# Batch 0's first heads and mixed k rows: the maximum as the bias of the exponentials, v only cast, and a new order

## The chip, the core and the metric

The kernel runs on one core of a Trainium2 chip. The metric is the device time of one launch in microseconds. The core's engines run side by side, each working through its own queue in order: TensorE (PE; its weight loads are listed as PEld), VectorE (DVE), ScalarE (ACT), GpSimd (POOL) and SyncE (SP), which only issues transfers. Matmul results land in PSUM, 8 banks of 128 x 512 fp32; the kernel numbers them 0 to 7.

## What is computed

Two stages. The first is an attention without a softmax over pairs: queries and keys are mapped by a small matrix to 128 features, and the features and their negatives go through an exponential, each row lowered by its largest absolute value. The second is a feed-forward with a gate.

```python
def phi(x):                                   # x: (8, 8, 576, 64), w_phi: (64, 128)
    proj = np.einsum('bhsd,df->bhsf', x, w_phi)
    proj = proj - np.max(np.abs(proj), axis=-1, keepdims=True)
    return np.concatenate([np.exp(proj), np.exp(-proj)], axis=-1)
q_p, k_p = (phi(q), phi(k))
kv = np.einsum('bhsf,bhsd->bhfd', k_p, v)
z = np.sum(k_p, axis=2)
num = np.einsum('bhsf,bhfd->bhsd', q_p, kv)
den = np.einsum('bhsf,bhf->bhs', q_p, z)[..., None] + 1e-06
attn = num / den
...
x = attn as (4608, 512)                       # tokens x (heads * 64)
gate = np.maximum(x @ w_gate, 0.0)            # (512, 1536)
val = x @ w_val                               # (512, 1536)
out = gate * val @ w_out                      # (4608, 512), fp32
```

In `phi`, one maximum m per row of k stands in both halves: exp(p - m) and exp(-p + m). Since these are factors of a whole row, exp(-m) and exp(m) may as well be multiplied onto the row of v that the row of k meets in `kv`.

## The kernel before

The program is a list of short steps, written out in the string `ORDER` (lines 17 to 256) and carried out word by word: `ke.0.1.3.0:6@kp1` is step ke with arguments 0, 1, 3, 0, PSUM bank 6, and buffer 1 of ring kp. The list's order is each engine's order; the engines meet only at the data and buffers that they share.

Batches are worked one after the other. Of each head's 576 rows, 512 are taken as four blocks of 128; the last 64 rows of all heads are the mixed rows. k is worked in three groups of heads, (0, 1), (2, 3, 4), (5, 6, 7), where the first group has the mixed rows in its free place. The feed-forward works on groups of 512 tokens: groups 0 to 7 for the batches, and group 8 for the mixed rows. There the steps are, with the lines of the profile:

- Loads: `lf` is the first k load; `lk`, `lq`, `lv`, `lm`, `lw` load k, q, v and their mixed rows (GpSimd issues those of k and q, and batch 0's v; SyncE issues the later v and the mixed v); `wl` (L532) loads a third of one feed-forward weight, wv or wg.
- k of batch b, group j, block i: features (`k3` or `kr`, L566), then `kx` (L670) takes the largest absolute value of each row on DVE, and `ke` (L662) the two exponentials on ACT, for all three heads at once, 384 columns, sign s = 0 or 1. `ke` does not lower by the maximum. Instead `kk` (L679) makes exp(-m) and exp(m) of the maxima (12 columns), and GpSimd multiplies v by both (`vs`, L719, with `vo` for the column of ones that gives z; `vq` for mixed rows).
- For batch 0's first group this is done on DVE and through PSUM: `kp` (L690) writes exp(-m) and exp(m) into a PSUM bank, `vd` (L700, two of them) multiplies v by them, `vp` (L709) writes the column of ones, and `vz` (L652, two of them) multiplies the mixed rows of v.
- `kv` (L768) are the products of k's exponentials and the scaled v; `kc` (L779) copies them out on ACT, once for each group of heads.
- q: features (`qb` or `qc`), exponentials `qe` (L843, ACT, 512 columns), and the maximum by `qx`, `qy`, `qz`, `qu` (DVE, with a transpose on TensorE) and `qw` (L884, ACT, a small exponential for each token block of batch 0).
- Output of attention for token block i, head group g: `nu` (L891, matmuls of 65 columns), `nt` and `nv` (L912, L922, DVE), the reciprocal `nr` (L930, DVE), and the normalization `nx` (L934, GpSimd).
- The transposed activations: for batch 0 by TensorE, `xp` (L971), and a copy, `xa` (L985, ACT) or `xc` (DVE); for later batches by a transposing transfer of SyncE.
- Feed-forward of group 0 in quarters: `pv`, `pg` (L1094), `pa` (L1109, ACT), `pb` (L1115, DVE). Of the others: `fv`, `fg` (L1065), `va` or `vb` (L1080, L1083), `ga` (L1086), and the output products `fo` (L1126), copied out by `oc` (L1135, ACT) or `oe` (DVE) and stored by `od`. One row block is done in halves at the end: `fp` (L1157), `o1` (L1166) and `d1` (L1173) on ACT, `o2`, `d2` on DVE and SyncE.
- `zz.N` (L429) are N matmuls of zeros into bank 7, whose result is not used.

## Time and profile before

| | |
|---|---|
| time, median of 3 runs | 372.36 us (372.12 to 373.22) |
| the profiled execution: its time | 371.86 us |
| the profiled execution: its span | 370.1 us |
| instructions | 9178 |
| PE busy | 362.3 us, 98% of the span |
| PEld busy | 196.8 us, 53% |
| DVE busy | 289.2 us, 78% |
| ACT busy | 227.1 us, 61% |
| POOL busy | 156.5 us, 42% |
| granted TensorE clock | 1.00 |
| HBM | 37.81 MB read, 9.44 MB written |

The span runs from the first to the last recorded instruction or transfer; 1.8 us of the execution lie around it. Ends of matmuls are modelled in the profile and matmuls overlap, so PE's busy time says how long some matmul was open. In a timeline the columns are start, duration, engine, line, operation and tiles, and how many instructions one row merges; in square brackets stands how long the engine was idle before and what ended it. A row of the waits reads: who, for whom; us in total, times, longest.

### The profile page before, as it was taken

The numbers are of one execution on the slowest core, as the hardware profiler recorded it, in microseconds if no ns is written. First come the engines' busy times: TensorE is split into PE (matmuls) and PEld (weight loads), VectorE is DVE, ScalarE is ACT, GpSimd is POOL, SyncE is SP. The second block draws the span as 40 slices with busy tenths as digits, with TensorE's granted clock in tenths as the row PEclk, the third lists the DMA queues.
The fourth block names the chain that finished last, engine by engine and source line by source line (L and its number), as shares of the span: only waits on it lengthen the run. The fifth ranks groups of instructions, "written<-read, shape, count | busy, mean of one in ns | idle before, by whom it ended". The sixth has DMA issues, their size and how long they took to land.

```text
span 370.1 us, 9178 instructions
## 1 busy us (share of the span) xinstructions
PE 362.3 (98%) x3573; PEld 196.8 (53%) x3624; DVE 289.2 (78%) x674; ACT 227.1 (61%) x550; POOL 156.5 (42%) x161
## 2 busy tenths in 40 slices
...
GB/s 144 253 197 196 178 186 142 182 16 171 135 108 123 158 130 76 83 173 100 58 102 116 14 144 57 46 113 58 126 69 15 2 73 97 47 0 25 33 28 142
DMA packets 90380, 38.09 MB, mean 103 GB/s; under 512 B 64226, under 2 KB 85602, under 8 KB 90338
## 3 DMA queue, kind: packets, MB, share of 16 engines
...
q8 instruction: 28, 0.46, 0.5%
q10 hardware_dynamic: 144, 0.13, 0.1%
...
HBM read 37.81 MB, written 9.44 MB: 128 GB/s over the span
## 4 chain that ended last, share of the span: by engine, by line
PE 87%; issue 4%; DVE 4%; POOL 2%; ACT 1%; DMA 1%; SPq 0%; POOLq 0%; ACTq 0%
PE bank L1065 43%; PE bank L1126 22%; PE bank L768 4%; PE bank L1094 4%; PE bank L891 4%; PE bank L566 2%; PE bank L828 2%; PE bank L429 2%; POOL xu L934 1%; ACT kp L662 1%; DVE h L851 1%; PE bank L1047 1%; PE bank L1157 1%; DMA xTs<-xu 1%; DVE kT L550 1%
## 5 line engine op out<-in xcount | busy, mean ns | idle before, releaser
L1126 PE MATMUL bank<-wo,h 128*128 128x512 bf16 x401 | 96.2, 379 | 1.1 <-issue 0.2
L662 ACT ACTIVATE kp<-bank 128x384 bf16<-128x384 f32 x192 | 84.4, 518 | 15.1 <-PE bank L566 10.1
L1080 ACT CAST val<-bank 128x512 bf16<-128x512 f32 x81 | 47.2, 595 | 73.7 <-PE bank L1065 65.1
L1086 DVE SCALAR_TENSOR_TENSOR h<-bank,val 128x512 bf16<-128x512 f32 x100 | 66.8, 678 | 28.1 <-PE bank L1065 14.2
L1065 PE MATMUL bank<-xTs,wv 128*128 128x512 bf16 x334 | 85.6, 379 | 0.8
L1065 PE MATMUL bank<-xTs,wg 128*128 128x512 bf16 x340 | 85.3, 379 | 0.6
L934 POOL TENSOR_TENSOR xu<-u,r 128x512 bf16<-128x512 f32 x36 | 37.2, 1041 | 96.0 <-DVE r L930 48.1
L843 ACT ACTIVATE qp<-bank 128x512 bf16<-128x512 f32 x128 | 69.2, 620 | 10.7 <-PE bank L828 9.4
L719 POOL TENSOR_TENSOR vs<-vn,ek 128x780 bf16<-128x780 f32 (+2 forms) x40 | 53.7, 1363 | 24.6 <-ACT ek L679 13.5
L1126 PEld LDWEIGHTS <-h 128*128 128x128 bf16 x420 | 39.1, 98 | 45.8 <-issue 2.4
L1065 PEld LDWEIGHTS <-wg 128*128 128x128 bf16 x400 | 37.4, 98 | 41.3 <-issue 0.7
L1065 PEld LDWEIGHTS <-wv 128*128 128x128 bf16 x400 | 36.9, 98 | 40.4 <-issue 0.7
L670 DVE TENSOR_REDUCE mk<-bank 128x3 f32<-128x384 f32 x96 | 49.6, 540 | 2.4 <-ACT kp L662 1.3
L851 DVE TRANSPOSE_TENSOR_REDUCE maxq<-bank 128x16 f32<-128x512 f32 x56 | 37.4, 692 | 6.1 <-ACT qp L843 3.3
L922 DVE TENSOR_TENSOR u<-bank,t 128x195 f32<-128x195 f32 (+1 forms) x108 | 33.8, 329 | 2.8 <-POOL xu L934 0.6
L912 DVE TENSOR_TENSOR t<-bank,cq 128x195 f32<-128x195 f32 (+1 forms) x96 | 30.1, 324 | 6.8 <-PE bank L891 5.9
L891 PEld LDWEIGHTS <-qp 128*128 128x128 bf16 x512 | 23.1, 98 | 12.6 <-issue 2.0
L891 PE MATMUL bank<-kv,qp 128*128 128x65 bf16 x512 | 26.1, 193 | 0.4 <-ACT kv L779 0.2
L1135 ACT COPY ob<-bank 128x512 f32<-128x512 f32 x19 | 11.3, 596 | 22.2 <-PE bank L1126 22.1
L747 POOL TENSOR_TENSOR vr<-vm,ek 64x520 bf16<-64x520 f32 x14 | 14.8, 1057 | 21.3 <-DMA vm<-in_v_dram 10.6
L1138 DVE COPY ob<-bank 128x512 f32<-128x512 f32 x16 | 11.0, 685 | 16.1 <-PE bank L1126 13.8
L768 PEld LDWEIGHTS <-kp 128*128 128x128 bf16 x640 | 21.6, 97 | 2.8 <-ACT qp L843 0.2
...
## 6 DMA issues: line engine op xcount, KB each, us to landing
out_dram<-ob SPq DMA_DIRECT2D x31, 256.0 KB, 2.4
vn<-in_v_dram SPq DMA_DIRECT2D x24, 256.0 KB, 4.4
...
out_dram<-ob SPq DMA_DIRECT2D x9, 128.0 KB, 2.3
```

The costliest lines, as they stand in the source:

```text
L662: nc.scalar.activation(kp_of(3 * b + j)[:, i, s].rearrange("p n f -> p (n f)"), bank[bk[0]][:, 0 : 3 * F], AF.Exp, scale=(1.0, -1.0)[s],)
L670: nc.vector.tensor_reduce(mk_of(3 * b + j)[:, :, i], bank[bk[0]][:, 0 : 3 * F].rearrange("p (n f) -> p n f", f=F), axis=AX.X, op=ALU.max, ...
L719: nc.gpsimd.tensor_tensor(vs_of(3 * b + j)[:, s, 0:n].rearrange("p n i e -> p (n i) e")[:, :, 0:e], src[:, lo:hi].rearrange("p h i e -> p ...
L768: nc.tensor.matmul(out_ps[:, h - lo, s, :], lhsT=lhsT, rhs=rhs, start=(at == 0), stop=(at == 2 * n * (C + 1) - 1),)
L843: nc.scalar.activation(qp_of(4 * b + i)[:, s, 4 * hq : 4 * hq + 4].rearrange("p h m -> p (h m)"), bank[bk[0]], AF.Exp, scale=(1.0, -1.0)[s],)
L851: nc.vector.tensor_reduce((maxq0[:, i] if b == 0 else maxq)[:, :, i, 4 * hq : 4 * hq + 4].rearrange("p t h -> p h t"), bank[bk[0]].rearran ...
L891: nc.tensor.matmul(bank[bk[0]][:, E * n : E * (n + 1)], lhsT=qp_of(4 * b + i)[:, s, h, :], rhs=kv_of(b)[:, h, s, 0:E],)
L934: eng.tensor_tensor(xu_of(n).rearrange("p (h d) -> p h d", d=D), u_of(n)[:, :, 0:D], r_of(n).to_broadcast([P, H, D]), op=ALU.mult,)
L1065: nc.tensor.matmul(bank[bk[0]], lhsT=w[:, dc, P * f : P * f + P], rhs=xT(g)[:, dc, :], start=(dc == 0), stop=(dc == NDC - 1),)
L1080: nc.scalar.copy(val_of(NFC * g + f), bank[bk[0]])
L1086: nc.vector.scalar_tensor_tensor(h2_of(g, f), bank[bk[0]], 0.0, val_of(NFC * g + f), op0=ALU.max, op1=ALU.mult)
L1126: nc.tensor.matmul(bank[bk[0]], lhsT=h2_of(g, f)[:, P * t : P * t + P], rhs=wo_sb[:, f, :], start=(f == 0), stop=(f == NFC - 1),)
```

## The change

For batch 0's first group of heads, with the mixed rows, the maximum goes into the exponentials themselves. `kb` (DVE) makes the negated maxima of the group, 12 columns. Each `ke` of the group becomes a `kz`: three exponentials on ACT, one for each head, 128 columns each, with the row's maximum as bias (-m with sign 0, m with sign 1). v of the group is then the same for both signs: `vc` (DVE) casts it once, `vi` (DVE) sets the column of ones, and `vk` (DVE, two of them) copies the mixed rows. `kp`, `vd`, `vp` and `vz` go. `kv` reads the one plane of v for both signs. Other groups and batches are computed as before.

The memset of the mixed v (`ms.2`) now covers two columns, the first of which the load `lw` of the mixed v then writes over, so that this load comes behind the memset; in the order it stands behind the fourth maximum of the second group. The whole list is in a new order. In it batch 0's v is loaded after all of its q and k; the v of batch 1 and the last third-loads of the weights (`wl`) stand elsewhere; `w1` and `wa`, which make a second form of the feature matrix, come later; the filler is 88 matmuls in 19 places instead of 85 in 22; and the last row block is `fo.7.0` with `oc` and `od` instead of the half block `fp.7.2.0` with `o1` and `d1`.

The list is shown to a little beyond the first `pv`, and at its end:

```diff
 ORDER = """
-ms.0 lf ms.2 lm.0.0 ms.4@vr0 ms.6 id lk.0.2 lk.0.0 wq ms.3@vr1 if ms.5 zz.15:7 kf.0:0 ms.9 kf.1:1
-zz.6:7 wd kh.0:0@kT0 sl k3.1.0:23 ke.0.1.0.0:2@kp0 w1:4 kg.1:1 kx.0.1.1:3@mk0 kx.0.1.0:2 wa:4 zz.2:7
-k3.1.1:56 ke.0.1.3.0:6 lm.0.1 kx.0.1.2:5 zz.3:7 k0.2:0 lq.0.1 ke.0.1.3.1:6 k1.2:0@kT1 ke.0.1.0.1:2
-zz.3:7 k0.0:1 ke.0.1.2.1:5 ke.0.1.1.1:3 k3.2.1:42 ke.0.1.2.0:5 kx.0.1.3:6 k1.0:1@kT2 zz.5:7
-k3.0.1:06 kk.0.1.0@ek0 k3.0.0:15 ke.0.1.1.0:3 ke.0.0.3.0:6@kp1 q0.1:3 lw.0.1 lq.0.0 kx.0.2.3:2@mk1
-kx.0.2.2:4 kk.0.1.1 ke.0.2.2.0:4@kp2 kx.0.0.0:1@mk2 kx.0.0.2:0 lv.0.1 ke.0.2.2.1:4 ke.0.0.1.1:5
-kx.0.0.3:6 q1.1:3@qT0 ke.0.0.1.0:5 ke.0.0.3.1:6 lv.0.0 zz.6:7 q0.0:4 kx.0.0.1:5 wl.0.1 zz.4:7
-k3.2.0:36 lv.0.2 ke.0.2.3.0:2 ke.0.0.2.1:0 ke.0.0.0.1:1 q1.0:4@qT1 ke.0.2.3.1:2 kx.0.2.1:6 zz.1:7
-qb.1.1:5 zz.3:7 qb.0.1:4 kx.0.2.0:3 ke.0.0.0.0:1 zz.2:7 qb.0.0:2 qx.0.0.1:4 ke.0.0.2.0:0 zz.1:7
-qb.1.0:1 qx.0.1.1:5 zz.7:7 qy.0.1:0 kp.0.0.0:2 ke.0.2.0.0:3 lk.1.3 kk.0.2.1@ek1 lw.0.0 kp.0.0.1:2
-kk.0.2.0 ke.0.2.1.1:6 vo.1@vs0 qx.0.1.0:1 qe.0.0.1.0:4@qp0 ke.0.2.0.1:3 qe.0.0.1.1:4 lq.1.2
-qe.0.1.0.0:1@qp1 qe.0.1.0.1:1 vs.0.1.0 qz.0.1:0@my0 zz.4:7 qb.0.3:0 qx.0.0.0:2 zz.2:7 qy.0.0:3
-vd.0.0.0:2@vs1 qz.0.0:3@my1 vs.0.1.1 qe.0.1.1.1:5 vp.0:2 qu.0.1@mz0 ke.0.2.1.0:6 qe.0.1.1.0:5 wl.0.0
-vz.0:2 qb.0.2:4 zz.2:7 qb.1.3:3 zz.2:7 qb.1.2:1 vd.0.0.1:2 qu.0.0@mz1 vz.1:2 qe.0.1.3.0:3@qp2
-vo.2@vs2 qw.0.0@cq0 qx.0.0.3:0 qx.0.0.2:4 qe.0.0.0.0:2 vs.0.2.1 zz.7:7 kv.0.0:6 qx.0.1.3:3 lw.1.1
-vs.0.2.0 kc.0.0:6@kv0 kt.1.1@kT3 qe.0.0.0.1:2 kv.0.2:5 kv.0.1:6 qe.0.0.2.1:4@qp3 lm.1.1 kc.0.2:5
-wl.1.1 kc.0.1:6 nu.0.0.0:2 nt.0.0.0:2@t0 zz.1:7 nu.0.0.2:5 qw.0.1 qx.0.1.2:1 qe.0.0.2.0:4
-qe.0.1.3.1:3 nu.0.0.1:6 nv.0.0.0:2@u0 zz.2:7 nu.0.1.2:4 lv.1.2 nu.0.1.0:2 qe.0.1.2.1:1 nt.0.0.1:6@t1
-lm.1.0 nt.0.0.2:5@t2 qy.0.2:3 nv.0.0.1:6 qe.0.0.3.0:0 nv.0.0.2:5 nt.0.1.0:2@t3 zz.2:7 nu.0.1.1:6
-qy.0.3:5 nr.0.0@r0 qe.0.1.2.0:1 qz.0.2:3@my2 nv.0.1.0:2@u1 qz.0.3:5@my0 qu.0.2@mz2 zz.5:7
-kr.1.1:3125 qe.0.0.3.1:0 nt.0.1.2:4@t0 nt.0.1.1:6@t1 qw.0.2 wl.1.0 nu.0.2.2:0 nx.0.0@xu0 nv.0.1.2:4
-xp.0.0:7 nv.0.1.1:6 nt.0.2.2:0@t2 ke.1.1.3.1:5@kp3 nr.0.1@r1 nu.0.2.1:4 xa.0.0:7 nt.0.2.1:4@t3
-nu.0.2.0:6 ke.1.1.0.1:3 nt.0.2.0:6@t0 qu.0.3@mz1 ke.1.1.0.0:3 pv.1.0:7 nv.0.2.1:4@u2 nv.0.2.2:0
-nv.0.2.0:6 nu.0.3.1:4 qw.0.3 ke.1.1.1.0:1 nx.0.1@xu1 kx.1.1.0:3@mk3 xp.0.1:0 pa.1.0:7@val0
-kx.1.1.3:5 pv.0.0:6 nr.0.2@r2 xa.0.1:0 nt.0.3.1:4@t1 nu.0.3.0:3 kx.1.1.1:1 nt.0.3.0:3@t3
+ms.0 ms.6 id ms.3@vr0 lf lk.0.0 wq ms.4@vr1 lm.0.1 sl if zz.15:7 kf.1:0 kf.0:1 lm.0.0 ms.9
+kg.1:0@kT0 kh.0:1 wd zz.6:7 k3.1.0:23 ms.5 zz.2:7 k3.1.1:45 lq.0.1 vi.0@vs0 ke.0.1.1.1:3@kp0 kx.0.1.0:2@mk0
+ke.0.1.1.0:3 ke.0.1.0.1:2 ke.0.1.3.0:5 kx.0.1.2:4 kx.0.1.1:3 lk.0.2 zz.4:7 k0.0:6 k1.0:6@kT1 lq.0.0
+kx.0.1.3:5 ms.2 lw.0.0 lw.0.1 zz.6:7 k3.0.0:01 kx.0.0.0:0@mk1 ke.0.1.2.1:4 k3.0.1:36 ke.0.1.2.0:4 kx.0.0.3:6
+ke.0.1.0.0:2 kk.0.1.1@ek0 zz.7:7 k0.2:4 kx.0.0.1:1 lv.0.1 ke.0.1.3.1:5 kz.0.0.0.1:0@kp1 kz.0.0.3.1:6
+q0.1:2 lv.0.2 kx.0.0.2:3 k1.2:4@kT2 kb.0 zz.4:7 k3.2.1:54 kk.0.1.0 kz.0.0.1.1:1 kz.0.0.2.1:3
+kz.0.0.2.0:3 q1.1:2@qT0 zz.3:7 q0.0:2 lv.0.0 kx.0.2.3:4@mk2 kx.0.2.2:5 qb.1.1:3 lm.1.1
+kz.0.0.0.0:0 q1.0:2@qT1 qx.0.1.1:3 kz.0.0.3.0:6 qb.1.0:0 ke.0.2.3.1:4@kp2 zz.4:7 k3.2.0:62 wl.0.1
+kz.0.0.1.0:1 ke.0.2.3.0:4 zz.3:7 qb.0.1:1 lk.1.3 kx.0.2.1:2 wl.0.0 ke.0.2.2.1:5 lm.1.0
+qe.0.1.0.1:0@qp0 kx.0.2.0:6 qx.0.0.1:1 ke.0.2.2.0:5 vk.1 kk.0.2.1@ek1 vc.0 lq.1.2 zz.10:7 qy.0.1:4
+qz.0.1:4@my0 qb.1.2:5 kk.0.2.0 qe.0.1.0.0:0 ke.0.2.0.1:6 ke.0.2.0.0:6 qx.0.1.0:0 qe.0.1.1.0:3@qp1
+qu.0.1@mz0 zz.3:7 qb.0.0:4 zz.3:7 qb.0.3:0 qe.0.0.1.1:1 qx.0.0.0:4 qe.0.0.1.0:1 qe.0.1.1.1:3
+ke.0.2.1.0:2 qb.1.3:6 qx.0.1.3:6 ke.0.2.1.1:2 vs.0.1.1@vs1 zz.8:7 qy.0.0:1 qx.0.1.2:5 qw.0.1@cq0
+qz.0.0:1@my1 vs.0.1.0 vs.0.2.0@vs2 qe.0.0.0.1:4 vo.1 qe.0.0.0.0:4 vk.0 zz.1:7 qb.0.2:3 lw.1.0
+qu.0.0@mz1 vo.2 vs.0.2.1 qx.0.0.3:0 kv.0.0:1 kc.0.0:1@kv0 qx.0.0.2:3 kv.0.1:2 qy.0.2:4
+qe.0.1.2.1:5@qp2 kv.0.2:1 qw.0.0 kt.1.1@kT3 qe.0.1.2.0:5 qz.0.2:4@my2 nu.0.0.0:4 kt.1.2@kT1
+nt.0.0.0:4@t0 kc.0.1:2 lw.1.1 qy.0.3:5 qz.0.3:5@my0 zz.1:7 nu.0.0.1:2 nv.0.0.0:4@u0 qu.0.2@mz2
+kc.0.2:1 qe.0.1.3.0:6@qp3 qw.0.2 lv.1.1 nt.0.0.1:2@t1 nu.0.0.2:5 nt.0.0.2:5@t2 nv.0.0.1:2 nu.0.1.1:1
+wl.1.1 nv.0.0.2:5 qu.0.3@mz0 nu.0.1.2:4 nr.0.0@r0 qe.0.0.2.1:3 nt.0.1.1:1@t3 nt.0.1.2:4@t0 zz.3:7
+nu.0.1.0:2 nv.0.1.1:1@u1 qe.0.0.2.0:3 qe.0.0.3.1:0 nt.0.1.0:2@t1 qe.0.0.3.0:0 w1:5 wa:5 nu.0.2.1:3
+nv.0.1.2:4 nv.0.1.0:2 zz.4:7 nu.0.2.0:1 nt.0.2.0:1@t2 nx.0.0@xu0 nt.0.2.1:3@t3 qe.0.1.3.1:6 qw.0.3
+zz.1:7 xp.0.0:7 kr.1.1:0542 xa.0.0:7 nu.0.3.2:6 nv.0.2.0:1@u2 nr.0.1@r1 nv.0.2.1:3 nt.0.3.2:6@t0
+nu.0.3.0:1 nu.0.2.2:7 ke.1.1.3.0:2@kp3 nt.0.2.2:7@t1 nv.0.3.2:6@u0 ke.1.1.0.0:0 ke.1.1.3.1:2
+nv.0.2.2:7 pv.0.0:3 nt.0.3.0:1@t2 ke.1.1.1.0:5 kx.1.1.3:2@mk3 nr.0.2@r2 nx.0.1@xu1 nv.0.3.0:1
+qt.1.1@qT2 nx.0.2@xu2 xp.0.1:6 ke.1.1.0.1:0 pv.1.0:7 kx.1.1.0:0 xa.0.1:6 nu.0.3.1:2 ke.1.1.1.1:5
+wl.1.0 pv.1.1:1 nt.0.3.1:2@t3 pa.1.0:7@val0 xp.0.2:6 pv.0.1:7 ln.0.0 pa.0.0:3@val1 kx.1.1.1:5
+nv.0.3.1:2 pa.1.1:1@val2 ku.1@kT2 ke.1.1.2.0:4 qc.1.1:3015 nr.0.3@r0 xa.0.2:6 nx.0.3@xu3 lm.2.0
 ...
-fo.7.0.1:2 fo.7.0.2:2 fp.7.2.1:0 oc.7.0:2@ob1 od.7.0 od.8.0 fo.7.1.0:4 fo.7.1.1:4 fo.7.3.2:1
-fo.7.1.2:4 oe.7.3:1@ob2 fp.7.2.0:6 od.7.3 oe.7.1:4@ob1 o2.7.2:0@ob0 od.7.1 d2.7.2 o1.7.2:6 d1.7.2
+ga.7.6:2@hs9 ga.7.11:7@hs7 fo.7.1.0:0 oe.8.1:4@ob0 od.6.0 fp.7.2.0:3 fo.7.1.1:0 o1.7.2:3@ob2 od.8.2
+oc.8.0:5@ob1 fo.7.3.0:6 d1.7.2 fo.7.3.1:6 fp.7.2.1:1 fo.7.3.2:6 o2.7.2:1 od.8.1 od.8.0 oe.7.3:6@ob0
+d2.7.2 fo.7.1.2:0 oe.7.1:0@ob1 od.7.1 fo.7.0.0:2 od.7.3 fo.7.0.1:2 fo.7.0.2:2 oc.7.0:2@ob2 od.7.0
 """
...
+    mneg = sb.tile([P, 3, 3, 4], FP32, name="mneg", tag="mneg")
...
+    BIASED = (0,)
...
-            2: lambda: nc.vector.memset(vm_of(0)[:, :, D : D + 1], 1.0),
+            2: lambda: nc.vector.memset(vm_of(0)[:, :, D - 1 : D + 1], 1.0),
...
+    def do_kb(bk, j):
+        nc.vector.tensor_scalar_mul(
+            mneg[:, j].rearrange("p n i -> p (n i)"), mk_of(j).rearrange("p n i -> p (n i)"), -1.0
+        )
+
+    def do_kz(bk, b, j, i, s):
+        for n in range(3):
+            nc.scalar.activation(
+                kp_of(j)[:, i, s, n],
+                bank[bk[0]][:, F * n : F * (n + 1)],
+                AF.Exp,
+                bias=(mneg[:, j] if s == 0 else mk_of(j))[:, n, i : i + 1],
+                scale=(1.0, -1.0)[s],
+            )
+
+    def cast_v(copy, j):
+        lo, hi = HEADS[j]
+        copy(
+            vs_of(j)[:, 0, 0 : hi - lo].rearrange("p n i e -> p (n i) e")[:, :, 0:D],
+            v_flat()[:, lo:hi].rearrange("p h i e -> p (h i) e"),
+        )
+
+    def do_vc(bk, j):
+        cast_v(nc.vector.tensor_copy, j)
...
+    def do_vi(bk, j):
+        n = HEADS[j][1] - HEADS[j][0]
+        nc.vector.memset(vs_of(j)[:, 0, 0:n].rearrange("p n i e -> p (n i) e")[:, :, D : D + 1], 1.0)
...
+    def do_vk(bk, hh):
+        r = slice(SM * hh, SM * (hh + 1))
+        nc.vector.tensor_copy(vr_of(0)[r, 0, :, hh, 0:E], vm_of(0)[r])
...
                 for i in range(C + 1):
                     if i < C:
                         lhsT = kp_of(3 * b + j)[:, i, s, 3 - n + h - lo, :]
-                        rhs = vs_of(3 * b + j)[:, s, h - lo, i, 0:E]
+                        plane = 0 if b == 0 and j in BIASED else s
+                        rhs = vs_of(3 * b + j)[:, plane, h - lo, i, 0:E]
                     else:
                         lhsT = kp_of(3 * b)[:, h // 2, s, 0, :]
-                        rhs = vr_of(b)[:, s, h // 2, h % 2, 0:E]
+                        rhs = vr_of(b)[:, s if b else 0, h // 2, h % 2, 0:E]
```

428 lines of the change are left out of this document (215 added, 213 removed).

## The prediction

> **What bounds the kernel now.** I read the page's chain that ended last first, then the busy time by stretches, then the waits of each engine inside a stretch, and last the timeline of the queue that the change loads.
>
> ```profile
> PE 87%; issue 4%; DVE 4%; POOL 2%; ACT 1%; DMA 1%; SPq 0%; POOLq 0%; ACTq 0%
> ```
>
> Over the whole span the chain is TensorE's. But the change sits in the first 25 us, so the stretches count more than the sums. Columns of the next rows: PE, PEld, DVE, ACT, POOL busy, granted clock, DMA share, GB/s.
>
> ```profile
> 0.00:10.00 10.00, 8.94 (x82) 6.57 (x84) 6.38 (x18) 5.03 (x12) 8.88 (x17) 1.00 0.97 149
> 10.00:20.00 10.00, 9.84 (x81) 5.54 (x76) 9.80 (x23) 9.96 (x29) 7.82 (x9) 1.00 1.27 248
> 20.00:28.00 8.00, 7.50 (x174) 6.36 (x172) 7.94 (x26) 7.71 (x20) 4.47 (x7) 1.00 1.28 197
> 28.00:40.00 12.00, 12.00 (x234) 11.24 (x234) 11.92 (x31) 11.80 (x29) 8.30 (x11) 1.00 1.09 185
> ```
>
> TensorE's busy share before 28 us is mostly the filler matmuls on zeros, so it says nothing there. ACT (9.96 of 10) and DVE (9.80 of 10) are both full from 10 to 20 us. Who waited, in three answers: ACT from 6.7 to 27.4 us, DVE from 6.7 to 25.6, PE's matmuls from 28 to 366:
>
> ```profile
> ACT kp L662 <- PE bank L642: 1.1, 1, 1.1
> ACT kp L662 <- PE bank L566: 0.2, 1, 0.2
> ```
>
> ```profile
> DVE my L869 <- PE bank L861: 0.2, 1, 0.2
> ```
>
> ```profile
> PE bank L1094 <- ACT xTs L985: 0.2, 1, 0.2
> PE bank L1126 <- issue: 0.2, 1, 0.2
> ```
>
> The 1.1 is before the first exponential. After it ACT waits 0.2 us until 27.4 and DVE 0.2 us until 25.6: two queues that run end to end. From 28 us on the matmuls wait 0.4 us in 338. So the time is (when TensorE gets its first feed-forward work) + (a fixed amount of matmul work without gaps) + (the tail). An edit at the start moves the end one for one, and the body has almost nothing to give.
>
> The first feed-forward matmuls (step pv) wait for the transposed activations that ACT copies out (xa.0.0). ACT's and TensorE's timelines at that place:
>
> ```profile
> 26.36 0.21 ACT L884 ACTIVATE cq<-mz 128x8 f32<-128x8 f32 x1
> 26.80 0.49 ACT L662 ACTIVATE kp<-bank 128x384 bf16<-128x384 f32 x1 [0.23 <-PE bank L566]
> 27.31 0.58 ACT L985 COPY xTs<-bank 128x512 bf16<-128x512 bf16 x1
> ```
>
> ```profile
> 27.95 1.05 PE L1094 MATMUL bank<-xTs,wv 128*128 128x128 bf16 x16 [0.24 <-ACT xTs L985]
> 28.84 0.34 PE L891 MATMUL bank<-kv,qp 128*128 128x65 bf16 x6
> ...
> 30.14 0.47 PE L891 MATMUL bank<-kv,qp 128*128 128x65 bf16 x10
> 30.44 0.22 PE L1094 MATMUL bank<-xTs,wv 128*128 128x128 bf16 x1
> ```
>
> **ACT, part by part.** The terms come from the groups on ACT between 6.7 and 27.3 us, and from its timeline:
>
> ```profile
> L662 ACT ACTIVATE kp<-bank 128x384 bf16<-128x384 f32 x25 | 10.5, 549 | 1.3 <-PE bank L642 1.1 <-PE bank L566 0.2
> ...
> L679 ACT ACTIVATE ek<-mk 128x12 f32<-128x12 f32 x4 | 0.9, 234 | 0.0
> ```
>
> ```profile
> 10.66 4.38 ACT L662 ACTIVATE kp<-bank 128x384 bf16<-128x384 f32 x11
> 15.08 0.18 ACT L690 ACTIVATE bank<-mk 128x12 f32<-128x12 f32 x1
> 15.20 0.47 ACT L662 ACTIVATE kp<-bank 128x384 bf16<-128x384 f32 x1
> ```
>
> Neighbours overlap, so a queue is priced by its step, not by the mean duration. Eleven exponentials of 384 columns take 4.38, one alone 0.47: the step is (4.38 - 0.47)/10 = 0.39. A 12-column one steps 15.20 - 15.08 = 0.12. Removed: 8 steps ke.0.0 x 0.39 = 3.12, and 2 steps kp x 0.12 = 0.24; together 3.36.
>
> Added: 8 steps kz, each three exponentials of 128 columns with a bias column, 24 in all. No exponential of before takes its bias from a tile, so this cost is bounded. Lower end, the overlapped step: 0.12 + 116 columns x (0.39 - 0.12)/372 = 0.20. Upper end, nothing overlapped: the means, 0.234 + 116 x (0.549 - 0.234)/372 = 0.33. I take 0.29, nearer to the upper end: each of the 24 must fetch its own column of maxima before its data can run, and the overlap that makes the lower end was seen only where nothing is fetched. 24 x 0.29 = 6.96 (ends 4.8 and 7.9). Net on ACT +3.6 (ends +1.4 and +4.5).
>
> The Trainium skill, page "ScalarE: Activation LUTs", section "What ACT_TABLE_LOAD costs", has a rule that speaks against this change: an ACTIVATE pays about 93 ns more for a bias read through a [128,1] pointer than for an immediate, on top of a fixed part and 0.833 ns per column, and neighbours overlap by about 93 ns. By its figures a kz exponential would be an estimated 0.29 us with the pointer and 0.20 without, and the net on ACT +3.7 or +1.4. No run here shows the pointer's part yet.
>
> Of what stands ahead of xa.0.0 on ACT, two things more change: batch 1's first exponential goes behind it (-0.39; it is the 25th of the group row), and the last of batch 0's four query scales (qw.0.3) goes ahead (+0.12). 3.6 - 0.27 = +3.3; the 0.2 that ACT waited at 26.80 is swallowed: **+3.1** (ends +0.9 and +4.0). w1 and wa are moved but stay ahead of xa.0.0: nothing.
>
> New waits on ACT: kz with sign 0 waits for kb (all four maxima, negated), with sign 1 for its own maximum; every later exponential queues behind. The order puts kk and ke.0.1 steps between and the sign-1 steps first, and a DVE maximum (0.55 in the first row below) is shorter than the three exponentials that it frees (0.87), so I cost it at nothing; if a maximum is late, one such step, 0.55.
>
> **DVE.** Groups of DVE from 6.7 to 25.5 us, and the reciprocal that opens the first normalization:
>
> ```profile
> L670 DVE TENSOR_REDUCE mk<-bank 128x3 f32<-128x384 f32 x12 | 6.0, 549 | 0.0
> ...
> L652 DVE TENSOR_TENSOR vr<-vm,bank 64x520 bf16<-64x520 f32 x2 | 1.4, 676 | 0.0
> L700 DVE TENSOR_TENSOR vs<-vn,bank 128x512 bf16<-128x512 f32 x2 | 1.3, 660 | 0.0
> ```
>
> ```profile
> 25.49 0.17 DVE L930 RECIPROCAL r<-u 128x8 f32<-128x8 f32 x1
> ```
>
> Removed 1.4 + 1.3 = 2.7 (and vp, a cast of 16 columns). Added: one cast of v (512 wide), two of 260 on 64 rows, one negation of 12. A cast is at most the multiply that it replaces (0.66, 0.68, 0.68) and none is under the 8-column reciprocal, 0.17, which I take for the negation: 0.7 to 2.2, and I take 1.3, near the middle, as the two narrow ones are half as wide as their multiply. So DVE is relieved by 1.4 (0.5 to 2.0). That is worth nothing on the path if ACT is 3 us behind: the second half of kv goes through ACT's copies (kc.0.1, kc.0.2), which stand behind all of the batch-0 exponentials, and the first ratio on DVE needs them. DVE's gain becomes idle time.
>
> **TensorE, GpSimd, loads.** Ahead of the first pv the new order has nu.0.3.2 and nu.0.3.0, 10 matmuls of 65 columns that before come after it: (30.44 - 30.14)/10 = 0.03 each, **-0.3**. Filler: 88 instead of 85, in idle time, nothing. After the first pv ACT does five k exponentials and xa.0.1 (5 x 0.39 + 0.58 = 2.5) while TensorE has two pv (27.95 to 28.84 is one, 0.9), the transposes and six nu matmuls (2.2): **+0.3** of idle that the row of before doesn't have. The v loads of batch 0 stand behind the same q and k loads in both orders; those of batch 1 feed only GpSimd. SyncE's load of the mixed v now waits for a memset behind four maxima on DVE (2.2 us of them); behind it on SyncE queue only mixed v and batch 1's v, and its reader stands eight maxima and four copies further on: nothing, unless it lands after DVE asks. GpSimd issues fifteen loads ahead of its four v multiplies; the groups of GpSimd up to 26.8 us:
>
> ```profile
> L719 POOL TENSOR_TENSOR vs<-vn,ek 128x768 bf16<-128x768 f32 x4 | 5.8, 1476 | 0.0
> L438 POOL DMA_DIRECT2D kn<-in_k_dram x3 | 2.5, 823 | 0.0
> ```
>
> 15 x 0.82 + 5.8 = 18, from some 2 us on: near 21, an estimate, while ACT's batch-0 work then runs to about 27. Nothing.
>
> **The tail.** Before, the last work is a 256-wide product, ACT's half copy and a 128 KB store; after, it is a full row block (fo.7.0, oc.7.0, od.7.0). ACT's last rows, and the stores issued after 300 us (KB, median us to landing):
>
> ```profile
> 360.85 0.58 ACT L1135 COPY ob<-bank 128x512 f32<-128x512 f32 x1 [3.73 <-PE bank L1126]
> 366.97 0.37 ACT L1166 COPY ob<-bank 128x256 f32<-128x256 f32 x1 [5.53 <-PE bank L1157]
> 367.37 0.37 ACTq L1173 DMA_DIRECT2D out_dram<-ob  x1
> ```
>
> ```profile
> out_dram<-ob SPq DMA_DIRECT2D x8, 256.0 KB, 2.2
> out_dram<-ob SPq DMA_DIRECT2D x9, 128.0 KB, 2.3
> out_dram<-ob ACTq DMA_DIRECT2D x1, 128.0 KB, 1.8
> ```
>
> The copy grows by 0.58 - 0.37 = 0.2, the store by up to 2.2 - 1.8 = 0.4: **+0.5** (0.2 to 0.6).
>
> **The sum.** +3.1 - 0.3 + 0.3 + 0.5 = +3.6 on the profiled execution's 371.86, that is 375.5. That execution lies 0.5 below the median of the three runs, 372.36; against the median the forecast is **376.0**, +1.0%. With kz at its ends the same sum is +1.4 and +4.5, 373.8 and 376.9. (About 0.3%, 1.1 us, is what a measurement of this kernel can tell from no change: 371.2 to 373.5.)
>
> **Rivals.** One: kz is cheap, 0.20, and ACT still paces. 373.8, right above the border of no change. For it: all ACT rows of before overlap well. Against: none of them reads a bias. 0.23.
>
> Two, the other side: ACT isn't what is late, DVE is, and the change relieves it. Place: the reciprocal at 25.49. DVE's queue ahead of it loses 1.4 and gains steps moved forward (one k transpose and the smaller max steps of two more token blocks, some 1.3), less one ratio; so it comes some 0.4 to 1.0 earlier, the first pv with it, no idle after it: -0.7 - 0.3 + 0.5 = -0.5, 371.9, and 371.0 with the small tail and the large relief. For it: DVE is as full as ACT (7.94 of 8 from 20 to 28). It decides only where the kz work costs no more than what it replaces less DVE's gain, 24 x 0.12 = 2.9, below the lower end of 0.20. 0.18, a part of which is that my reading of the ACT queue is wrong.
>
> Three: the forecast, and a weight load comes late too. The last third of wv:
>
> ```profile
> 35.35 0.82 POOL L532 DMA_DIRECT2D wv<-in_moe_w_val_dram  x1
> ```
>
> ```profile
> DMA to landing us min/median/max: 6.4/8.0/11.0
> ```
>
> ```profile
> 44.39 1.03 PE L1065 MATMUL bank<-xTs,wv 128*128 128x512 bf16 x3
> ```
>
> Its first reader came 9.0 after the issue. In the new order three more load issues (0.7 each) stand between the last normalization of batch 0 and this one, so 6.9 remain, against a landing of 8.0 in the median: a wait of 1.1 (none to 4), 377.1. 0.13.
>
> **How the numbers follow.** Forecast 0.46, one 0.23, two 0.18, three 0.13. Faster by over 0.3%: two thirds of rival two, 0.12. Within 0.3%: the rest of it and 0.09 of rival one, 0.15. Slower: 0.73. The range reaches from rival two's 372.0 (leaving out its faster part) to 377.6, the forecast with kz at 0.33 and half of rival three's wait; some 0.07 lies above.
>
> **What would show it.** Right: the kz step from a run of them, 0.27 to 0.31; ACT without waits until xa.0.0, which starts near 30.4; DVE with some 2 to 3 us of waits for PE and ACT between 7 and 28; first pv near 31; matmul waits after it under 1.5; a last ACT copy of 0.58. Wrong: kz steps near 0.20 (rival one); xa.0.0 at or before 27.3 with ACT waiting (rival two); a wait for wv near 47 us (rival three); matmul waits of several us in the body, which none of my terms holds.

## The result and the profile after

The changed kernel takes 374.99 us (median of 6 executions, 373.75 to 376.12), the kernel before 372.44 beside it (6 executions, 371.95 to 373.22): a ratio of 1.0072 [1.0059, 1.0086]. The profiled execution took 374.90 us, its span is 373.1. That is slower, as forecast (376.0), and inside the range. But the experiments below show that the size came out right with a part of the working wrong: a second limit, VectorE's casts against GpSimd, lies right behind ScalarE's longer queue, and the queues that the prediction priced one by one hold each other up. The prediction had neither.

The page's chain that ended last, first part, and the busy time of two stretches (PE, PEld, DVE, ACT, POOL busy, granted clock, DMA share, GB/s):

```profile
PE 94%; ACT 2%; DVE 2%; issue 1%
```

```profile
10.00:20.00 10.00, 8.33 (x66) 4.68 (x64) 7.98 (x14) 10.00 (x36) 7.86 (x8) 0.83 1.25 241
20.00:28.00 8.00, 7.35 (x135) 5.58 (x135) 7.88 (x23) 6.97 (x18) 2.47 (x4) 1.00 1.34 205
```

By the chain TensorE looks even more like the limit than before (94% for 87%), and again the start decides. ScalarE is full from 10 to 20 us, as before. Two things are new: VectorE has 2.0 us of idle time there, and TensorE's granted clock is 0.83, where the kernel before had 1.00 all through. The longest waits of ACT, DVE and PE between 6.7 and 28 us, and of PE from 28 to 370:

```profile
ACT kv L822 <- DVE h L894: 0.9, 1, 0.9
```

```profile
DVE mk L712 <- PE bank L644: 1.4, 2, 1.1
DVE h L894 <- PE bank L857: 0.8, 2, 0.6
```

```profile
PE bank L857 <- ACT kp L670: 1.4, 2, 1.0
```

```profile
PE bank L1169 <- issue: 0.6, 4, 0.2
```

A ring can be read out of the first three: TensorE's query matmuls (L857) wait for PSUM banks that the new exponentials (L670) hold, VectorE waits for TensorE, and ScalarE's copy of kv waits for VectorE. After 28 us nothing waits to speak of. The first feed-forward matmuls start here:

```profile
30.88 1.05 PE L1137 MATMUL bank<-xTs,wv 128*128 128x128 bf16 x16
```

30.88 against 27.95, 2.93 later, while the profiled executions differ by 3.04. What follows the first pv takes 374.90 - 30.88 = 344.02 us here and 371.86 - 27.95 = 343.91 before. In all twelve kernels below it is 343.97 to 344.5. So all but some 0.6 us of any difference in this document is made ahead of the first pv.

### The profile page after: what moved, and what is told of

It reads as the page before. It is cut to its first block, busy times and chain, and to the rows that moved or that the text cites. A ratio compares the mean times of both kernels' runs of the same rounds, so it can differ in the third digit from the quotient of the medians.

```text
span 373.1 us, 9209 instructions
## 1 busy us (share of the span) xinstructions
PE 362.9 (97%) x3575; PEld 196.8 (53%) x3627; DVE 287.5 (77%) x674; ACT 229.9 (62%) x564; POOL 156.2 (42%) x161
## 4 chain that ended last, share of the span: by engine, by line
PE 94%; ACT 2%; DVE 2%; issue 1%
PE bank L1108 46%; PE bank L1169 24%; PE bank L811 5%; PE bank L934 4%; PE bank L1137 4%; PE bank L568 3%; PE bank L871 2%; PE bank L431 2%; ACT kp L670 1%; DVE h L894 1%; ACT kp L704 1%; PE bank L1200 1%; PE bank L1090 1%; PE bank L857 0%; DVE vs L680 0%
## 5 line engine op out<-in xcount | busy, mean ns | idle before, releaser
L1169 PE MATMUL bank<-wo,h 128*128 128x512 bf16 x402 | 97.4, 379 | 1.3 <-issue 0.6
L704 ACT ACTIVATE kp<-bank 128x384 bf16<-128x384 f32 x184 | 83.2, 534 | 11.7 <-PE bank L568 8.4
L1108 PE MATMUL bank<-xTs,wg 128*128 128x512 bf16 x339 | 86.3, 379 | 0.7
L886 ACT ACTIVATE qp<-bank 128x512 bf16<-128x512 f32 x128 | 71.3, 658 | 8.6 <-DVE maxq L894 5.3
L811 PE MATMUL bank<-vs,kp 128*128 128x65 bf16 x512 | 22.3, 193 | 0.1
L811 PE MATMUL bank<-vr,kp 128*128 128x65 bf16 x128 | 20.3, 193 | 0.0
```

What stands on the lines that cost most here:

```text
L704: nc.scalar.activation(kp_of(3 * b + j)[:, i, s].rearrange("p n f -> p (n f)"), bank[bk[0]][:, 0 : 3 * F], AF.Exp, scale=(1.0, -1.0)[s],)
L811: nc.tensor.matmul(out_ps[:, h - lo, s, :], lhsT=lhsT, rhs=rhs, start=(at == 0), stop=(at == 2 * n * (C + 1) - 1),)
L886: nc.scalar.activation(qp_of(4 * b + i)[:, s, 4 * hq : 4 * hq + 4].rearrange("p h m -> p (h m)"), bank[bk[0]], AF.Exp, scale=(1.0, -1.0)[s],)
L1108: nc.tensor.matmul(bank[bk[0]], lhsT=w[:, dc, P * f : P * f + P], rhs=xT(g)[:, dc, :], start=(dc == 0), stop=(dc == NDC - 1),)
L1169: nc.tensor.matmul(bank[bk[0]], lhsT=h2_of(g, f)[:, P * t : P * t + P], rhs=wo_sb[:, f, :], start=(f == 0), stop=(f == NFC - 1),)
```

## The experiments

Four theories met in the first four runs. One: ScalarE's queue got longer, and sets the first pv. Two: VectorE is late, through the cast of v. Three: the fall of TensorE's clock costs the time. Four: the new order costs it, whatever the method. This table holds all twelve runs; each time is a median of 4 to 12 executions, each ratio is to the kernel before on the same chip, and the last three columns are of the profiled execution (its time, the start of its first pv, its mean granted clock).

| kernel | us | ratio [95%] | profiled us | first pv | clock |
|---|---|---|---|---|---|
| before | 372.44 | | 371.86 | 27.95 | 1.000 |
| changed | 374.99 | 1.0072 [1.0059, 1.0086] | 374.90 | 30.88 | 0.995 |
| old_method | 375.89 | 1.0095 [1.0067, 1.0123] | 376.82 | 32.85 | 0.990 |
| one_wide | 378.30 | 1.0155 [1.0130, 1.0180] | 378.53 | 34.53 | 0.990 |
| vc_mult | 375.40 | 1.0078 [1.0050, 1.0106] | 374.39 | 30.15 | 1.000 |
| more_filler | 374.48 | 1.0063 [1.0039, 1.0088] | 374.33 | 30.32 | 0.999 |
| early_lw | 374.78 | 1.0058 [1.0037, 1.0078] | 374.78 | 30.80 | 0.995 |
| early_lw_one_wide | 377.44 | 1.0138 [1.0118, 1.0157] | 377.40 | 33.41 | 0.991 |
| early_lw_old_method | 375.62 | 1.0081 [1.0062, 1.0101] | 375.59 | 31.62 | 0.995 |
| one_wide_filler | 375.96 | 1.0097 [1.0075, 1.0118] | 375.52 | 31.53 | 0.998 |
| pool_casts | 375.70 | 1.0096 [1.0083, 1.0109] | 376.18 | 31.77 | 0.995 |
| pool_casts_no_bias | 372.37 | 1.0004 [0.9992, 1.0015] | 372.15 | 27.64 | 0.999 |
| pool_casts_one_wide | 372.14 | 0.9997 [0.9988, 1.0006] | 371.72 | 27.61 | 1.000 |
| early_lw_old_method_2 | 376.90 | 1.0120 [1.0096, 1.0144] | 375.81 | 31.84 | 0.994 |

The profiled executions also differ in when ScalarE's row of exponentials begins: at 6.42 to 7.38 us, and by 0.75 us between pool_casts (7.38) and pool_casts_no_bias (6.63), whose lists are the same. So a difference of half a us between two first pvs says little.

### The old method in the new order (old_method)

In ORDER, up to kv.0.0, every kz becomes ke; further:

```diff
- kb.0
+ kp.0.0.0:6 kp.0.0.1:6
- vk.1 kk.0.2.1@ek1 vc.0
+ kk.0.2.1@ek1 vd.0.0.0:6@vs0 vd.0.0.1:6 vp.0:6 vz.1:6 vz.0:6
- vi.0@vs0
- vk.0
-    BIASED = (0,)
+    BIASED = ()
-                        rhs = vr_of(b)[:, s if b else 0, h // 2, h % 2, 0:E]
+                        rhs = vr_of(b)[:, s, h // 2, h % 2, 0:E]
```

> The changed kernel's order, with the old method in it: the 24 exponentials with a bias (0.25 us each in the changed kernel's trace, 6.0 us) become 8 of 384 columns and two of 12 (8 x 0.39 + 2 x 0.12 = 3.36 us), and the casts of v become the two multiplications, the copy of the factors and the two mixed multiplications. Theory 1 (ScalarE's queue is what was lengthened): first pv 2.6 us earlier, near 28.2 us, and the whole near 372.3 us, like the kernel before. Theory 2 (VectorE was late, through the 1.71 us cast): VectorE's sum in the stretch hardly falls (1.71 + 0.57 against 2 x 0.65 + some 1.0), so at most the 0.6 us of ScalarE's wait goes: 374.4. Theory 4 (the new order itself, not the method): 375.0, no change.

375.89 us: not back at 372. But the run is no clean test of the order, since it brought a wait of its own. ScalarE's and TensorE's longest waits:

```profile
ACT kp L704 <- DVE vr L654: 2.9, 1, 2.9
```

```profile
PE bank L857 <- DVE my L912: 2.4, 1, 2.4
```

The exponentials of the third heads read the same PSUM bank (6) that I had given the factors, and stood behind the multiplications there. The last run below takes this up.

### One wide exponential (one_wide)

```diff
     def do_kz(bk, b, j, i, s):
-        for n in range(3):
...
+        nc.scalar.activation(
+            kp_of(j)[:, i, s].rearrange("p n f -> p (n f)"),
+            bank[bk[0]][:, 0 : 3 * F],
+            AF.Exp,
+            scale=(1.0, -1.0)[s],
+        )
```

> Leaves out the maximum: each group of three 128-column exponentials with a bias becomes one of 384 columns without. All else, VectorE's work included, is as in the changed kernel. ScalarE's queue loses 24 x 0.25 - 8 x 0.39 = 2.9 us. Theory 1: first pv between 28.0 and 28.8 us, time 372.2 to 373.0, with VectorE's lateness perhaps keeping some of it. Theory 2: ScalarE's wait for kv's copy grows from 0.85 to over 2.5 us and the time falls by under 0.8 (374.2 or more). Theory 3 (the TensorE clock that falls to half between 15 and 19 us is what costs): the banks come free earlier, the gap in TensorE's work shrinks, and the time falls by 1.2 if the clock comes back to 1.00, by nothing if not.

Every theory missed: with 2.9 us less on ScalarE the kernel became 3.3 us slower (378.30). VectorE's and GpSimd's timelines, and TensorE's, show why:

```profile
18.17 2.27 DVE L699 CAST vr<-vm 64x260 bf16<-64x260 f32 x1 [2.48 <-DMA vm<-in_v_dram]
20.47 0.43 DVE L678 CAST vs<-vn 128x512 bf16<-128x512 f32 x1
```

```profile
14.23 4.34 POOL L759 TENSOR_TENSOR vs<-vn,ek 128x768 bf16<-128x768 f32 x3
18.51 0.42 POOL L771 CAST vs<-ek 128x24 bf16<-128x24 f32 x2
18.82 1.46 POOL L759 TENSOR_TENSOR vs<-vn,ek 128x768 bf16<-128x768 f32 x1
```

```profile
16.38 0.50 PE L431 MATMUL bank<-zero 128*128 128x256 bf16 x3
21.15 0.58 PE L855 MATMUL bank<-qT,w 64*128 64x512 bf16 x1 [4.26 <-DVE my L910]
```

```profile
17.00:21.00 4.00, 0.00 (x0) 0.00 (x0) 2.80 (x3) 2.37 (x6) 4.00 (x6) 1.00 1.37 201
...
22.00:28.00 6.00, 6.00 (x50) 3.48 (x49) 4.28 (x9) 1.65 (x5) 0.00 (x0) 0.50 1.29 190
```

VectorE's first mixed cast waits 2.48 us for its load; then it takes 2.27 us, a cast that takes 0.30 in the changed kernel, and ends at 20.44, just after GpSimd's last multiplication (20.28). TensorE, whose next query matmul is behind VectorE, idles 4.26 us, and then its clock is 0.50 from 22 to 28 us, just when the work for the first pv is due.

### The cast as a multiplication (vc_mult)

```diff
- vc.0
+ vw.0:6 vc.0:6
+    def do_vw(bk, j):
+        n = HEADS[j][1] - HEADS[j][0]
+        nc.vector.memset(bank[bk[0]][:, 3 * F : 3 * F + 4 * n], 1.0)
     def do_vc(bk, j):
-        cast_v(nc.vector.tensor_copy, j)
+        lo, hi = HEADS[j]
+        n = hi - lo
+        nc.vector.tensor_tensor(
+            vs_of(j)[:, 0, 0:n].rearrange("p n i e -> p (n i) e")[:, :, 0:D],
+            v_flat()[:, lo:hi].rearrange("p h i e -> p (h i) e"),
+            bank[bk[0]][:, 3 * F : 3 * F + 4 * n, None].to_broadcast([P, 4 * n, D]),
+            op=ALU.mult,
+        )
```

> The cast of v for the first heads becomes a multiplication by ones that lie in PSUM (a small fill of 8 columns ahead of it), so that VectorE reads one operand from PSUM as the old multiplications did. Theory 2 in its form of a conflict with GpSimd: 0.65 us in place of 1.71, VectorE 0.9 us earlier, ScalarE's wait for kv's copy 0.85 down to 0.25 or less, first pv 0.6 earlier, time 374.4. If the cast was slow for another reason (where v lies, the 16-bit output): it stays above 1.3 us and the time at 375.0. Theory 1 alone, with the wait worth nothing: 375.0 whatever the cast takes. Theory 3: 375.0.

First the rows of the changed kernel, VectorE and GpSimd, then those of this one:

```profile
18.04 0.30 DVE L701 CAST vr<-vm 64x260 bf16<-64x260 f32 x1
18.37 1.71 DVE L680 CAST vs<-vn 128x512 bf16<-128x512 f32 x1
```

```profile
18.32 1.47 POOL L761 TENSOR_TENSOR vs<-vn,ek 128x768 bf16<-128x768 f32 x1 [1.45 <-ACT ek L721]
```

```profile
18.46 0.69 DVE L692 TENSOR_TENSOR vs<-vn,bank 128x512 bf16<-128x512 f32 x1
```

```profile
18.28 1.47 POOL L772 TENSOR_TENSOR vs<-vn,ek 128x768 bf16<-128x768 f32 x1 [0.69 <-ACT ek L732]
```

Beside the same GpSimd multiplication the cast takes 1.71 us and the multiplication that reads one operand from PSUM takes 0.69. The conflict with GpSimd is shown. In time it brought little: first pv 0.73 earlier, in a profile whose clock stayed at 1.000, the median not lower (375.40, of executions at 374.2 to 374.8 with the clock at 0.999 or 1.000, and at 376.0 to 376.2 with 0.991 to 0.995). The run is not quite clean: the ones lie in PSUM bank 6, which the third heads' last exponentials need, and ScalarE waited 0.55 us for the multiplication at 19.25. Still, nothing here shows the slow cast to be the cost of the change, and early_lw below, where the cast took 0.43, says the same.

### More filler (more_filler)

```diff
- kx.0.2.2:5 qb.1.1:3
+ kx.0.2.2:5 zz.9:7 qb.1.1:3
- kz.0.0.3.0:6 qb.1.0:0
+ kz.0.0.3.0:6 zz.4:7 qb.1.0:0
```

> Thirteen more filler matmuls (nine and four of 256 columns, some 1.4 us) in the gaps of TensorE near 13 and 14.3 us, where it waits for banks that the new exponentials hold. Theory 3: the granted clock stays at 1.00 over 10 to 20 us (0.83 in the changed kernel) and the time falls by about 1.2 us to 373.7, like the one run of it at clock 1.0. Theory 1: TensorE is not what is late before first pv, so the clock there costs nothing: 375.0, give or take 0.3.

The clock from 10 to 20 us came back, VectorE's cast began 0.07 ahead of GpSimd's multiplication, and ran in 0.43 us; it was GpSimd that took longer, 1.68 for 1.46:

```profile
10.00:20.00 10.00, 9.47 (x88) 6.05 (x86) 8.10 (x18) 10.00 (x37) 7.26 (x7) 1.00 1.25 240
```

```profile
18.84 0.43 DVE L680 CAST vs<-vn 128x512 bf16<-128x512 f32 x1
```

```profile
18.91 1.68 POOL L761 TENSOR_TENSOR vs<-vn,ek 128x768 bf16<-128x768 f32 x1 [1.43 <-ACT ek L721]
```

In these rows the one that started first kept its pace, and the other paid. The time is 374.48: 0.5 lower, with overlapping intervals, where theory three wanted 1.2. (In the profile the exponentials began at 7.09 for 6.47 in the changed kernel; counted from there, first pv comes 1.2 us sooner. So theory three is not refuted here.) Over the executions of the changed kernel, early_lw, vc_mult and this one, those at a clock of 0.998 or more took 373.55 to 374.94, those at 0.995 or less 374.78 to 377.26: a stretch at half clock goes with 1 to 2 us. But at full clock the new method still stands at 373.55 or more, 1.75 above the fastest of before (371.80).

### Early loads of v's mixed rows (early_lw)

```diff
- ms.0 ms.6 id
+ ms.0 ms.2 ms.6 id
- wq ms.4@vr1
+ wq lw.0.1 lw.0.0 ms.4@vr1
- kx.0.1.3:5 ms.2 lw.0.0 lw.0.1 zz.6:7
+ kx.0.1.3:5 zz.6:7
```

> Only the loads of v's mixed rows move: their memset comes second on VectorE, and both loads stand behind w_phi on SyncE's queue as in the kernel before, so that they are issued near 2 us and not at 9.06 and some 6 us later. The new method and the rest of the order stay. Theory 1 (ScalarE's longer queue sets first pv, and the first theory's rivals are silent): no change, 375.0, within 0.4. Theory 5, formed after the last runs (two limits lie side by side: ScalarE's queue, and VectorE's queue that cannot go past the mixed cast before v's mixed rows land near 18 us): ScalarE is still as long, so 374.4 to 375.0 here too; what tells them apart is the next two runs. A cost of the earlier loads to the first loads of k: up to 0.3 later at the first exponential (6.47 us).

374.78, no change that can be told. Here too the cast of v met a free GpSimd (it began at 18.40, GpSimd at 18.55) and took 0.43.

### Early loads and one wide exponential (early_lw_one_wide)

Both edits above.

> Leaves out the maximum as the run with one wide exponential did, with the early loads of v's mixed rows beside it. Theory 5: with both limits taken away VectorE does not wait for the load (2.5 us in the run with late loads), TensorE does not idle 4.3 us near 17 to 21, its clock stays at 1.00, and first pv falls from 33.1 to 28.5 or less; time 372.0 to 373.0. If the load was not what mattered (only the clock, or the order): over 376.

Theory five falls: 377.44, 2.7 slower than with the early loads alone. (Where the expectation has 33.1 for the first pv of one_wide, the table has 34.53.) VectorE no longer waits for the load, and gains nothing by it:

```profile
15.87 4.40 DVE L699 CAST vr<-vm 64x260 bf16<-64x260 f32 x1
20.30 0.43 DVE L678 CAST vs<-vn 128x512 bf16<-128x512 f32 x1
```

```profile
14.06 4.33 POOL L759 TENSOR_TENSOR vs<-vn,ek 128x768 bf16<-128x768 f32 x3
18.34 0.42 POOL L771 CAST vs<-ek 128x24 bf16<-128x24 f32 x2
18.65 1.46 POOL L759 TENSOR_TENSOR vs<-vn,ek 128x768 bf16<-128x768 f32 x1
```

The cast starts 2.3 us earlier and ends at nearly the same place, 20.27, again just behind GpSimd's row of multiplications (20.11). A cast of 0.30 us takes 4.40. The rest of the study rests on this row: GpSimd's instructions follow each other without a gap, and VectorE does not come in between them. In the changed kernel there was a gap, since ScalarE was late: GpSimd waited 1.45 us there for ScalarE's factors (the bracket in its row above), and the mixed cast fell into it. With the faster ScalarE the gap is gone. TensorE again idles behind VectorE (3.94 us), and runs at a clock of 0.50 from 19 to 25 us.

The Trainium skill, page "SBUF — State Buffer", section "SBUF: two separate sides", says that VectorE and GpSimd share a pair of SBUF ports under an exclusive lock, taken by VectorE operations in a two-port mode or with two SBUF inputs, and that who starts first keeps it for the whole instruction. The rows agree on the kinds (the PSUM multiplication passes, the cast is blocked; in which mode the cast runs no row shows), and go further: the blocked cast waited through five instructions of GpSimd (three multiplications, two small casts), not one.

### Early loads and the old method (early_lw_old_method)

The edits of old_method and of early_lw.

> The changed kernel's order with the old method, and the early loads of v's mixed rows. Theory 5: VectorE's mixed multiplications no longer wait for the load, ScalarE's wait behind them (2.9 us) goes, first pv near 28.3, time 372.0 to 373.0, like the kernel before: the order costs little once the loads are early. Theory 4 (the order itself costs): 375 or more.

375.62. The wait for the load is gone, ScalarE's wait behind the multiplications (2.4 us) is not, so this run settles nothing on the order either.

### One wide exponential with filler (one_wide_filler)

```diff
- qu.0.1@mz0 zz.3:7 qb.0.0:4
+ qu.0.1@mz0 zz.36:7 qb.0.0:4
```

> Leaves out the maximum as the run with one wide exponential did, loads late as in the changed kernel, and 33 more filler matmuls of 256 columns (some 3.5 us) where TensorE idled 4.26 us ahead of a q matmul at 21.15. It tells what the halved clock adds behind such an idle stretch: in the run without, TensorE ran at 0.50 from 21 to 28 us. If the clock is most of its 3.3 us over the changed kernel: clock 1.00, first pv near 31.0 and time 375.0 to 375.8. If the late load alone does it: over 377.

375.96, a little above the 375.0 to 375.8 of the expectation, and 2.3 us less than without the filler, with nothing of the real work touched; VectorE's cast still ended at 20.26. TensorE's clock from 20 to 28 us, and its first pv, 3.0 us earlier than in one_wide:

```profile
20.00:28.00 8.00, 7.38 (x133) 5.55 (x132) 7.85 (x22) 4.34 (x12) 1.03 (x2) 1.00 1.33 205
```

```profile
31.53 1.05 PE L1135 MATMUL bank<-xTs,wv 128*128 128x128 bf16 x16
```

So the halved clock behind the idle stretch is worth 2.3 us in one_wide, which lies 3.3 over the changed kernel (and that one has a stretch at half clock of its own). The Trainium skill, page "TensorE: Matmul & The Clock Gate", section "Part 1: The HAM clock gate", has the clock fall to half after an idle window of some 3.4 us. The idle 4.26 us of one_wide agree. In old_method 2.38 us were enough (the clock was 0.54 at 19 to 20 us with TensorE idle from 17.40 to 19.78), and in the changed kernel it fell at 15 us without any idle stretch over 1.1 us, after three microseconds at a busy share of 0.72, 0.24 and 0.60.

### The casts on GpSimd (pool_casts)

The edit of early_lw, and:

```diff
- vk.1 kk.0.2.1@ek1 vc.0
+ kk.0.2.1@ek1
- vs.0.1.0 vs.0.2.0@vs2
+ vs.0.1.0 vg.0 vh.1 vh.0 vs.0.2.0@vs2
- vk.0
```

> The changed kernel with its exponentials with the maximum as bias kept; the early loads of v's mixed rows; and the casts of v (first heads, mixed rows) on GpSimd in place of VectorE, in the place where GpSimd waited 1.45 us for ScalarE. In every profile so far the time is first pv plus 344.0 us, so first pv is what is predicted. Theory 1 (ScalarE's queue, 2.65 us longer, is a limit by itself): VectorE is relieved, ScalarE's wait for kv's copy goes, first pv 30.0 to 30.4, time 374.0 to 374.4. Theory 6 (the limit is the pair of VectorE's casts and GpSimd's multiplications, which do not run at the same time): with no cast left on VectorE first pv would fall towards 28.3, time 372.3.

375.70: theory six alone falls (it wanted 372.3), and theory one's 374.0 to 374.4 was too low. On GpSimd the casts cost 0.61 us and, the two mixed ones, 0.88. ScalarE's, VectorE's and TensorE's waits from 6 us on:

```profile
ACT kv L822 <- DVE h L894: 0.8, 1, 0.8
```

```profile
DVE mk L712 <- PE bank L644: 2.0, 2, 1.1
DVE my L912 <- PE bank L904: 1.7, 1, 1.7
DVE h L894 <- PE bank L857: 1.3, 4, 0.6
```

```profile
PE bank L857 <- ACT kp L670: 1.8, 3, 1.1
```

It is the ring of the changed kernel again, now without any cast in it: banks held by the new exponentials, TensorE waiting and its clock at 0.86 over 10 to 20 us, VectorE waiting 5.0 us for TensorE, ScalarE 0.8 for VectorE.

### The casts on GpSimd, and no bias (pool_casts_no_bias)

The edit of pool_casts, and

```diff
-                bias=(mneg[:, j] if s == 0 else mk_of(j))[:, n, i : i + 1],
```

> As the run with the casts on GpSimd, and the bias left out of the 24 exponentials (leaves out the maximum): it prices the bias as a step of three 128-column exponentials with and without one (0.25 us each in the changed kernel). If the bias costs nothing: 0.25 again, first pv as in the run with the casts on GpSimd. If the step falls to 0.20: ScalarE's queue is 1.2 us shorter, and by theory 1 first pv and the time fall by as much (373.0); by theory 6 nothing changes.

372.37: the bias alone is worth 3.3 us in this setting. ScalarE's rows of three-part exponentials, in the changed kernel and then here:

```profile
9.57 1.71 ACT L670 ACTIVATE kp<-bank,mk 128x128 bf16<-128x128 f32 x6
11.08 0.30 ACT L721 ACTIVATE ek<-mk 128x12 f32<-128x12 f32 x1
11.19 1.75 ACT L670 ACTIVATE kp<-bank,mk 128x128 bf16<-128x128 f32 x6
12.69 2.57 ACT L670 ACTIVATE kp<-bank,mneg 128x128 bf16<-128x128 f32 x9
```

```profile
9.72 1.19 ACT L670 ACTIVATE kp<-bank 128x128 bf16<-128x128 f32 x6
10.68 0.32 ACT L720 ACTIVATE ek<-mk 128x12 f32<-128x12 f32 x1
10.78 2.77 ACT L670 ACTIVATE kp<-bank 128x128 bf16<-128x128 f32 x15
13.13 0.81 ACT L703 ACTIVATE kp<-bank 128x384 bf16<-128x384 f32 x1
```

Six with a bias go from 9.57 to 11.08, a step of 0.25; fifteen without go from 10.78 to 13.13, 0.157. The bias from a tile costs 0.09 us each, 24 x 0.094 = 2.3 in all. The Trainium skill, page "ScalarE: Activation LUTs", section "What ACT_TABLE_LOAD costs", has 93 ns for it: the trace agrees, where the prediction had no run for it. Leaving out the bias also frees the exponentials from waiting for the maxima, but that is not what helped: in pool_casts the only wait of ScalarE that the profile shows after its first exponential is the 0.8 us above, ahead of a copy of kv. That 2.3 us on ScalarE move the time by 3.3 fits the ring: TensorE's wait for banks is gone, the clock is 1.00 from 10 to 28 us, VectorE waits 0.9 us instead of 5.0.

### The casts on GpSimd, and one wide exponential (pool_casts_one_wide)

The edits of pool_casts and of one_wide.

> As the run with the casts on GpSimd, and each group of three exponentials made one of 384 columns without bias (leaves out the maximum). ScalarE's queue is 2.9 us shorter than in the changed kernel, and no VectorE cast can be held up by GpSimd. Theory 6 joined to theory 1 (with ScalarE relieved, GpSimd's multiplications close up and hold VectorE's cast for up to 4.40 us; without that cast nothing holds): no wait of VectorE over 1 us after 15 us, TensorE does not idle near 17 us, clock 1.00, first pv 27.5 to 28.5, time 371.5 to 372.5. If it stays over 376, the cast was not the cause either.

372.14, ratio 0.9997 to before, first pv 27.61: as expected. The longest waits of ScalarE and VectorE between 6.7 and 28 us:

```profile
ACT kp L702 <- PE bank L644: 0.7, 1, 0.7
```

```profile
DVE my L910 <- PE bank L902: 0.5, 1, 0.5
```

With three runs above this closes a square, all four with the early loads:

| | casts on VectorE | casts on GpSimd |
|---|---|---|
| kz, three with a bias | 374.78 | 375.70 |
| one wide, no bias | 377.44 | 372.14 |

Either cure alone leaves the kernel where it was, or slower; both together bring back the time of the kernel before. There are two limits, and each by itself is enough to keep the time up. And the new order alone is not the cost, since this kernel has it too.

### The old method again (early_lw_old_method_2)

The edits of early_lw_old_method, with ke.0.2.0.1:6 and ke.0.2.0.0:6 put ahead of vd.0.0.0.

> The changed kernel's order with the old method and the early loads, as the run before it, with one mend: the last two exponentials of the third heads stand ahead of the multiplications by the factors, which lie in the same PSUM bank, so that ScalarE does not wait 2.4 us for them. The old multiplications read the factors from PSUM and took 0.65 us each beside GpSimd's. Theory 1 and 6: no long wait left on ScalarE or VectorE, first pv 27.8 to 28.8, time 371.8 to 372.8, like the kernel before. Theory 4 (the new order is itself slower): 374 or more.

376.90, as theory four alone allowed (374 or more). Nothing of the new method is left in this kernel, ScalarE's work is that of before, and the first pv still comes at 31.84. But the mend has a price too: the multiplications now wait 0.7 us for the exponentials that stand ahead of them in the same bank. The longest waits of ScalarE and TensorE:

```profile
ACT kv L822 <- PE bank L811: 2.8, 1, 2.8
```

```profile
PE bank L857 <- DVE my L912: 2.6, 1, 2.6
```

TensorE idles at the same query matmul as in one_wide, behind a VectorE whose old multiplications (2 x 0.65 + 2 x 0.70 + 0.22 = 2.9 us) stand ahead of the query maxima, where the casts without a conflict are 0.43 + 2 x 0.28 = 1.0. So the new order is not neutral: it needs a VectorE that is quick at that place. In the kernel before, the same multiplications are spread between other VectorE work from 17.44 to 20.51 us; whether such a place in the new order would do wasn't tried, nor what the new method costs in the old order.

## Why the prediction was right, and where it was not

What the runs leave standing: ScalarE's longer queue is a limit (theory one; with the casts out of the way, 2.3 us of bias less on ScalarE bring 3.3 us). VectorE's casts against GpSimd are a second one behind it (theory two, in the form of a conflict): in the changed kernel itself it costs nothing that can be told (in early_lw the cast took 0.43, and the time stayed), but it bites as soon as ScalarE is quick. The halved clock (theory three) follows the idle time that either makes and adds to it: 1 to 2 us between executions of the new method, 2.3 in one_wide. The order (theory four) is not neutral, but not the cost by itself either (pool_casts_one_wide has it). The late loads (theory five) were not it.

**Where the time is made: right.** The time is the first pv plus a constant; the matmul waits after it are 0.6 us. First pv near 31 was forecast, it is 30.88.

**The kz term: right in kind, 0.04 us too dear each.** The step was put at 0.29 in 0.20 to 0.33, and is 0.25: 6.0 us and not 6.96, net 24 x 0.25 - 3.36 = +2.6 for +3.6. 24 x 0.04 = 0.96 us is about the forecast's excess on the median, 376.0 against 374.99, but that the two agree is luck: the forecast also missed the terms below, which partly cancel.

**"ACT without waits until xa.0.0": wrong by one wait.** xa.0.0 starts at 30.00, 2.69 later than before. ScalarE's two rows there, in the changed kernel:

```profile
24.13 0.38 ACT L822 CAST kv<-bank 128x260 bf16<-128x260 f32 x1 [0.85 <-DVE h L894]
...
30.00 0.63 ACT L1028 COPY xTs<-bank 128x512 bf16<-128x512 bf16 x1
```

The ledger of ScalarE's queue: +2.6 of kz, -0.27 by the two moved steps as forecast, +0.62 as this wait of 0.85 takes the place of the 0.23 before, -0.26 since the first exponential started that much earlier (6.47 for 6.73), together +2.7.

But the wait of 0.85 says more than its size: at 24.13, the first copy of kv, ScalarE was not the last to be ready, VectorE was. From that copy to xa.0.0 it is 5.87 us here, and 5.84 to 5.88 in ten of the thirteen kernels with the new order (5.56 to 6.16 in all), so nearly all that these kernels differ by comes about ahead of it. Ahead of it, the chain of work that leads to the first pv runs over ScalarE only until 14.49 us, and from then on over TensorE and VectorE alone. Nor could a ScalarE that was free sooner have started xa.0.0 more than 0.04 us sooner. What it copies hangs on VectorE's first reciprocal, over GpSimd's normalization and the transposes (L1014), which end at 29.96:

```profile
28.19 0.19 DVE L973 RECIPROCAL r<-u 128x8 f32<-128x8 f32 x1
28.46 1.04 POOL L977 TENSOR_TENSOR xu<-u,r 128x512 bf16<-128x512 f32 x1 [5.99 <-DVE r L973]
29.56 0.40 PE L1014 MATMUL bank<-ident,xu 128*128 128x128 bf16 x4
30.34 0.68 PE L934 MATMUL bank<-kv,qp 128*128 128x65 bf16 x16
```

The reciprocal comes 2.70 later than the 25.49 of before, xa.0.0 2.69. In twelve of the thirteen kernels with the new order first pv follows it by 2.69 to 2.70 us (2.93 in more_filler). So two roads reach xa.0.0 together, ScalarE's queue and VectorE's, and the new exponentials delay both: one directly, the other by the banks that they hold.

**"DVE's gain becomes idle time", worth nothing: half wrong.** The idle time came (2.2 us of waits for TensorE, as forecast). But the cast of v was priced at 0.66 at most, "the multiply that it replaces", and took 1.71: the old multiplication read PSUM and passed GpSimd by, the cast does not. The operation meant to be cheaper was the dearer one. The step that failed is the reading that only ScalarE was late: the prediction sums queues one by one, and has no term for banks that one engine holds and another waits for, nor for two engines that exclude each other. The sum stood, since ScalarE's queue is as late as VectorE's road, and late enough to open a gap for one of the casts. That one queue alone gave the size is in part luck; that the time comes back once ScalarE's work is taken away is false (one_wide, 378.30).

**TensorE's filler "says nothing": wrong.** It holds the clock. The new exponentials hold PSUM banks, TensorE waits 1.4 us for them, and falls to half clock from 15.2 to 18.6 us. One execution of the changed kernel kept the clock at 1.000 and took 373.75; those at 0.995 took 374.9 to 375.3, the one at 0.989 took 376.12.

**The mixed loads "nothing, unless it lands after DVE asks":** in the changed kernel VectorE got there at 18.01 and did not wait; vc_mult waited 0.5 and one_wide 2.48. The condition was named; with the early loads (early_lw) it is worth nothing.

**The tail: right.** The last copy takes 0.59, and from its start to the end of the span it is 3.55 us for 3.13 before, +0.4. **The nu steps, -0.3:** from the first pv to that copy's start it is 338.67 for 339.02, which agrees with that gain; of the idle time after the first pv (+0.3) nothing is seen. But the ten nu matmuls moved ahead are not free there: they are among the 16 in the row at 30.34 above, which keep TensorE busy until the first pv at 30.88, 0.25 us after the end of the copy that it needs (30.63); before it was 0.06. That is most of what takes 2.69 at xa.0.0 to 2.93 at the first pv, and the prediction has no term for it.

```profile
369.55 0.59 ACT L1178 COPY ob<-bank 128x512 f32<-128x512 f32 x1 [7.36 <-PE bank L1169]
```

**The rivals.** One (kz at 0.20) and three (a wait for wv) did not come: no such wait is in the trace. Two (VectorE is late, and relieved) named the right place, the reciprocal, which is as late as ScalarE's queue; but VectorE was not relieved, and the sign is wrong. (In the range, kz at 0.33 and half of rival three's wait add up to 376.9 + 0.55 = 377.4, not 377.6; nothing hangs on it.)

What stays open: how the 2.9 us split between ScalarE's queue and the ring behind it. The bounds are 1.75 (the fastest execution of the new method at full clock, 373.55, over the fastest of before, 371.80) and the whole. Why pool_casts is 0.9 slower than early_lw, with the same exponentials and a freer VectorE, is not settled either; between the two profiled executions 0.67 of the 0.97 us is a later first exponential (7.38 for 6.71).
